# Last pass of an attention backward: every slab product is ordered behind a store copy on VectorE

## The chip, the cores and the metric

The kernel runs on one core of a Trainium2 chip. TensorE (PE), VectorE (DVE), ScalarE (ACT), GpSimd (POOL) and SyncE (SP) each run their own instructions in order; data moves between HBM and the on-chip memory through 16 DMA engines. In this kernel SP's queue issues all loads and POOL's queue all stores. The metric is the device time of one execution in microseconds (us); three executions of the kernel before took 1945.61, 1946.26 and 1947.33 us, median 1946.26.

## The reference

One token passes through two identical layers, each an attention over a long cache and a dense block; then the gradients of all inputs are computed from `grad_out`.

```python
# A: 32 query heads, 4 key/value groups, 65536 cached positions, head size 128, x of 1024
q = (x @ wq);  scores = q @ k.T * Dh**-0.5;  p = softmax(scores);  o = p @ v;  return o @ wo
# B: squared ReLU
h = x @ w1 + b1;  r = max(h, 0);  return (r*r) @ w2 + b2

x = x + A(layernorm(x));  x = x + B(layernorm(x))
x = x + A(layernorm(x));  x = x + B(layernorm(x))
out, vjp = jax.vjp(f, A_x, A_k_cache, A_v_cache, A_wq, A_wo, B_w1, B_b1, B_w2, B_b2)
return (out, *vjp(grad_out))
```

The gradients of the two caches are as large as the caches themselves: 64 MB each in bfloat16. The same weights and caches serve both layers, so the gradients of the two layers are summed.

## The kernel before, in words

The kernel makes four passes over the caches: two forward (one for each layer), one backward for the later layer, and a last one (`attn_bwd4`, L1289) that does the backward of the earlier layer together with the cache gradients of both. Dense stages lie between. Only the last pass is touched by the change.

The last pass goes through 256 items, 64 for each of the four groups; an item (`c8`) is 8 chunks of 128 positions. Four items make a block of 32 chunks, 1 MB of K or V. A block lies in one slot of an arena of 20 slots in on-chip memory (`Slot`, L318). Which slot a block, a weight slab or a staged output gets is decided when the program is written out; a load into a slot waits, in SP's queue, for the last reader of what lay there.

For each item the stages of the pipeline (L1476) do the following. `vT` (L1337) transposes V on PE and copies the result out (`kt`, mostly DVE). `vS` (L1365) multiplies it with the output gradients and, once per block, DVE writes the product `X` (L1403). `eT` and `xT` transpose the weights and `X` (`xt`). `dV8` and `dK8` call `outer16` (L1418): two outer products into PSUM (`ps_gg`), each of which `evac` (L150) copies into the staged output slot, by a running estimate of load on ACT (L161) or on DVE (L164); when the slot is full, POOL issues the store. These copies are called store copies here. `k8` (L1445) multiplies K with `X`. The first seven V blocks are already transposed from the pass before, so the transposes of V run over the other 228 items.

Beside this runs background work (`Background`, L777): the other outer products of the weight gradients, and `g_rowdots` (L577), a product of a weight slab with a vector. It comes six times in this pass, each for one group: three times on `wo` (for the output gradient of the next group) and three times on `wq` (a part of the gradient of x). Each needs two loads of 1 MB, four slab rows in each; a slab row is multiplied on DVE with the vector spread over all partitions (L598, a "product": 48 in the pass), and ACT sums the result (L587). The products are numbered 1 to 48 here, so that each job has eight, the first four on its first slab and the next four on its second one. As written, the second slab is requested after the fourth product, and eight waiting steps (one for each item) come before the fifth:

```python
            elif kc % 4 == 0:
                for _ in range(steps):
                    yield "wait"
            t = mvs.tile([P, n], BF, name="mv_t", tag="mv_t", bufs=2)
            nc.vector.tensor_tensor(out=t[:, :], in0=slab, in1=vbc[:, :], op=ALU.mult)
```

The order on the engines in the last pass isn't the order of writing. The earlier passes are issued as written (`manual_schedule`, L1177 and L1284), but the last pass is left to a scheduler, which orders each engine's instructions when the program is built, by its own estimate of when operands are ready. So it can place a product earlier among DVE's instructions than it was written, if by that estimate its slab has landed and DVE is free. On the chip each engine then keeps to the built order and waits at an instruction whose operand isn't there.

Of the kernel before, what the change touches and what calls it, by code (L numbers as in the profile page):

```python
# [3 lines left out]

# [9 lines left out]
ALU = mybir.AluOpType  # L14
# [6 lines left out]
def kernel(  # L21
# [24 lines left out]
    nc = tc.nc  # L46
# [98 lines left out]
    def add_load(act=0.0, dve=0.0, pe=0.0):  # L145
        load["act"] += act
        load["dve"] += dve
        load["pe"] += pe

    def evac(out, in_, kind="bf"):  # L150
        n = 1
        for d in in_.shape[1:]:
            n *= d
        ca = 0.17 + n * 0.00083
        cd = 0.13 + n * (0.00105 if kind == "f32" else 0.00054)

        if PS["pass4"] and kind == "bf":
            ca += 1.5
        if kind == "kta" or kind != "kt" and load["act"] + ca <= load["dve"] + cd:
            load["act"] += 0.17 + n * 0.00083  # L160
            nc.scalar.copy(out=out, in_=in_)  # L161
        else:
            load["dve"] += cd
            nc.vector.tensor_copy(out=out, in_=in_)  # L164


    def col_from_dram(v1d, n, name):
        nj = n // P
        rows = tmp.tile([nj, P], BF, name="rows_c", tag="rows_c")
        nc.sync.dma_start(out=rows[:], in_=v1d.rearrange("(j p) -> j p", p=P))  # L170
        pt = ps_mv([P, nj], BF)
        nc.tensor.transpose(pt[:, :], rows[:, :], ident_b[0:nj, 0:nj])
        col = vec.tile([P, nj], F32, name=name)
        nc.vector.tensor_copy(out=col[:], in_=pt[:])
        return col
# [383 lines left out]
    def g_bcast_vec(vcol, nj):  # L559
        pt = ps_mv([nj, P], F32)  # L560
        nc.tensor.transpose(pt[:, :], vcol, ident_f[:, :])
        yield
        rows = tmp.tile([32, P], BF, name="bc_rows")
        nc.vector.tensor_copy(out=rows[0:nj, :], in_=pt[:, :])
        vbc = mvs.tile([P, nj * P], BF, name="vbc", tag="vbc", bufs=1)
        yield
        for j0 in range(0, nj, 4):
            pg = ps_gg() if PS["pass4"] else ps_tr([P, 512], F32)
            for jj in range(4):
                nc.tensor.matmul(pg[:, jj * P:(jj + 1) * P], lhsT=ident_b[0:nj, j0 + jj:j0 + jj + 1].to_broadcast([nj, P]),  # L570
                                 rhs=rows[0:nj, :], start=True, stop=True)
            nc.scalar.copy(out=vbc[:, j0 * P:(j0 + 4) * P], in_=pg[:, 0:512])
            add_load(act=0.6)
            yield
        return vbc

    def g_rowdots(slab_it, nk, vcol, nj, finish, name):  # L577
        n = nj * P
        y = vec.tile([P, nk], F32, name=name)
        nc.gpsimd.memset(y[:], 0.0)  # L580
        vbc = None
        due = None
        steps = 8 if PS["pass4"] else WAIT_STEPS

        def total(t, kc):
            def f():
                nc.scalar.activation(out=t[:, :], in_=t[:, :], func=ACTF.Copy, accum_out=y[:, kc:kc + 1])  # L587
            return f
        for kc, slab in slab_it:
            if vbc is None:  # L590
                vbc = yield from g_bcast_vec(vcol, nj)
                for _ in range(steps - WAIT_STEPS + 1):
                    yield "wait"
            elif kc % 4 == 0:
                for _ in range(steps):
                    yield "wait"
            t = mvs.tile([P, n], BF, name="mv_t", tag="mv_t", bufs=2)
            nc.vector.tensor_tensor(out=t[:, :], in0=slab, in1=vbc[:, :], op=ALU.mult)  # L598
            add_load(dve=0.1 + n * 0.00054, act=0.42 + n * 0.00083)
            if due is not None:  # L600
                due()
            due = total(t, kc)
            yield
        due()
        yield
        r = finish(y[:, :])
        if r is not None:
            yield from r
        yield
# [679 lines left out]
    def attn_bwd4(p, La, Lb, on_group, bg, stack, end=()):  # L1289
# [128 lines left out]
        def outer16(name, out, key, xt, gg, j1):  # L1418

            if j1 == 0:  # L1420
                state[key] = Slot(name, True)
            stg = state[key].t[:, :].rearrange("p (j d) -> p j d", d=DH)
            for m in range(2):
                pg = ps_gg()
                for h in range(2):
                    nc.tensor.matmul(pg[:, 512 * h:512 * h + 512], lhsT=xt[64 * h:64 * h + 64, j1 // 8 + m, :],  # L1426
                                     rhs=gg[64 * h:64 * h + 64, :, :].rearrange("p a b -> p (a b)"),
                                     start=True, stop=True, tile_position=(64 * h, 0))
                jj = j1 + 8 * m
                evac(stg[:, jj:jj + 8, :].rearrange("p j d -> p (j d)"), pg[:, :], kind="f32")  # L1430
            if j1 + 16 == J:
                nc.gpsimd.dma_start(out=out, in_=stg)
                state.pop(key).free(stored=True)
# [522 lines left out]
```

## Time and profile before

| | |
|---|---|
| median of three executions | 1946.26 us |
| profiled execution, its time and its span | 1939.92 us, 1938.1 us |
| busy: PE, DVE, ACT, POOL | 1585.2, 1170.3, 1044.9, 142.2 us |
| bytes through the DMA engines | 787.63 MB, mean 406 GB/s |
| last pass, about | 1214 to 1938 us of the span |
| products in the last pass | 48, median 681 ns |
| DVE idle before products in the last pass | 34.1 us, of which 33.3 us on slabs |
| loads of one block in the last pass, issue to landing | K 15.9 us, V 13.2 us (medians) |

Times in the profile's rows count from the start of the span. In a row of the timeline the first two numbers are start and duration; "L598" is the line in the kernel; what stands in square brackets is the time for which the engine did nothing before this instruction, and what ended that. "issue" there means that the profile shows no data that came in; where a wait on a semaphore stands in the queue ahead of the instruction, the idle time is that wait's. In a table of windows a row gives, for each engine, busy time and instructions, then the granted TensorE clock, the share of the 16 DMA engines that was busy, and GB/s.

### The profile page before, as it was taken

Reading aid. Unit: us, or ns where it says so; the run is one execution under the profiler, and the core shown is the slowest. Engines: PE = TensorE matmul, PEld = TensorE weight load, DVE = VectorE, ACT = ScalarE, POOL = GpSimd, SP = SyncE. Lnnn points to the kernel's source line nnn. Section 1 sums busy time; section 2 is a strip of 40 time slices with the busy share of each in tenths; the row PEclk is TensorE's granted clock in tenths of the full one; section 3 lists DMA queues with packets and bytes.
Section 4 is the critical chain, followed back from the end, with each engine's and each line's share of the span. In section 5 each row is a group of like instructions: output and inputs, shape, how many; then the busy total and the mean of one; then the engine's idle time right before and its main releaser. Section 6 shows DMA issues by size and latency. Waiting matters only on the chain. (4 is left out here: it accounts for less than half of the span.)

```text
span 1938.1 us, 66986 instructions
## 1 busy us (share of the span) xinstructions
PE 1585.2 (82%) x30199; PEld 1301.4 (67%) x30199; DVE 1170.3 (60%) x2453; ACT 1044.9 (54%) x1617; POOL 142.2 (7%) x321
## 2 busy tenths in 40 slices
PE   6878778688777888977787898889997987697987
PEld 6878777678777877877776886555554654454554
DVE  5655555255555554545454567777775886685876
ACT  3444334245433545445363455766875885575775
POOL 0000000000000000000000001121111211121211
PEclk9999899689999999998899999898997998797998
DMA  9999999999999998999999988999999999899998
GB/s 393 427 425 425 429 427 415 391 407 423 427 425 429 428 422 309 377 425 429 426 424 421 408 314 308 425 424 389 425 424 413 419 424 424 345 419 397 424 422 352
DMA packets 107149, 787.63 MB, mean 406 GB/s; under 512 B 9440, under 2 KB 16622, under 8 KB 42222
## 3 DMA queue, kind: packets, MB, share of 16 engines
q1 hardware_dynamic: 82782, 617.65, 77.2%
q0 software_dynamic: 24080, 165.70, 20.5%
q8 instruction: 236, 3.87, 0.7%
q14 instruction: 51, 0.42, 0.1%
HBM read 617.62 MB, written 165.69 MB: 404 GB/s over the span
## 5 line engine op out<-in xcount | busy, mean ns | idle before, releaser
L164 DVE COPY kt<-ps_tr 128x1024 bf16<-128x1024 bf16 x724 | 496.3, 688 | 429.0 <-PE ps_tr L1024 244.0
L161 ACT CAST arena<-ps_gg 128x1024 bf16<-128x1024 f32 x457 | 444.4, 1011 | 185.0 <-PE ps_gg L1426 137.9
L1024 PE MATMUL ps_tr<-ident_b,arena 128*128 128x128 bf16 x3840 | 308.2, 225 | 36.9 <-DMA arena<-in_A_k_cache_dram 27.5
L161 ACT COPY kt<-ps_tr 128x1024 bf16<-128x1024 bf16 x164 | 171.0, 1046 | 186.1 <-PE ps_tr L1216 103.3
L164 DVE CAST arena<-ps_gg 128x1024 bf16<-128x1024 f32 (+2 forms) x186 | 222.2, 1195 | 77.1 <-PE ps_gg L1426 34.5
L1024 PEld LDWEIGHTS <-arena 128*128 128x128 bf16 x3840 | 232.9, 101 | 44.7 <-DMA arena<-in_A_k_cache_dram 30.3
L1126 PE MATMUL ps_acc<-arena 128*128 128x64 bf16 (+4 forms) x4096 | 205.6, 196 | 60.2 <-DMA arena<-in_A_v_cache_dram 45.1
L1426 PE MATMUL ps_gg<-GG,xt 64*128 64x512 bf16 x1024 | 210.6, 409 | 43.3 <-DVE arena L164 28.3
L1345 PE MATMUL ps_tr<-ident_b,arena 128*128 128x128 bf16 x1824 | 177.4, 232 | 33.7 <-DMA arena<-in_A_v_cache_dram 30.7
L1126 PEld LDWEIGHTS <-arena 128*128 128x128 bf16 x4096 | 159.9, 100 | 66.1 <-DMA arena<-in_A_v_cache_dram 48.7
L1042 PE MATMUL ps_sc<-L_qpad,kt 128*128 128x64 bf16 (+7 forms) x3584 | 183.0, 194 | 16.3 <-issue 8.3
L1107 ACT ACTIVATE arena<-S_sb,L_negm 128x128 bf16<-128x128 f32 x256 | 165.5, 1002 | 55.7 <-DVE L_negm L1092 42.2
L1216 PE MATMUL ps_tr<-ident_b,arena 128*128 128x128 bf16 x1920 | 154.3, 226 | 44.3 <-DMA arena<-in_A_v_cache_dram 43.5
L1345 PEld LDWEIGHTS <-arena 128*128 128x128 bf16 x1824 | 116.8, 103 | 90.7 <-issue 55.2
L1042 PEld LDWEIGHTS <-kt 128*128 128x128 bf16 x3584 | 152.6, 100 | 20.2 <-issue 8.8
L1216 PEld LDWEIGHTS <-arena 128*128 128x128 bf16 x1920 | 117.1, 101 | 48.8 <-DMA arena<-in_A_v_cache_dram 46.1
L1457 PEld LDWEIGHTS <-arena 128*128 128x128 bf16 x2048 | 92.2, 101 | 57.8 <-issue 39.9
L1107 ACT ACTIVATION_READ_ACCUMULATOR arena<-S_sb,L_negm 128x1 f32 x256 | 127.9, 500 | 0.0
L1426 PEld LDWEIGHTS <-xt 64*128 64x128 bf16 x1024 | 64.5, 94 | 90.1 <-issue 52.3
L587 ACT ACTIVATE mv_t<-mv_t 128x1024 bf16<-128x1024 bf16 x96 | 102.1, 1065 | 35.8 <-DVE mv_t L598 35.8
L1382 PE MATMUL ps_sc<-DOB,kt 128*128 128x64 bf16 (+3 forms) x1824 | 112.3, 197 | 0.1
L1270 PE MATMUL ps_acc<-dsT,arena 128*128 128x64 bf16 (+7 forms) x2048 | 103.1, 194 | 11.3 <-DMA arena<-in_A_k_cache_dram 7.8
(317 smaller groups left out, 2154.0 us busy)
## 6 DMA issues: line engine op xcount, KB each, us to landing
arena<-in_A_k_cache_dram SPq DMA_DIRECT2D x82, 2048.0 KB, 21.7
arena<-in_A_v_cache_dram SPq DMA_DIRECT2D x79, 2048.0 KB, 21.7
out_dram<-arena POOLq DMA_DIRECT2D x149, 1024.0 KB, 16.2
arena<-in_A_v_cache_dram SPq DMA_DIRECT2D x84, 1024.0 KB, 14.2
arena<-in_A_k_cache_dram SPq DMA_DIRECT2D x84, 1024.0 KB, 14.6
arena<-in_A_wo_dram SPq DMA_DIRECT2D x22, 1024.0 KB, 19.6
arena<-in_B_w_dram SPq DMA_DIRECT2D x21, 1024.0 KB, 9.2
arena<-in_A_wq_dram SPq DMA_DIRECT2D x18, 1024.0 KB, 18.0
```

Of the source, the lines that this page charges most:

```text
L161: nc.scalar.copy(out=out, in_=in_)
L164: nc.vector.tensor_copy(out=out, in_=in_)
L587: nc.scalar.activation(out=t[:, :], in_=t[:, :], func=ACTF.Copy, accum_out=y[:, kc:kc + 1])
L1024: nc.tensor.transpose(pt[:, i, :], kb8[:, i, :], ident_b[:, :])
L1042: nc.tensor.matmul(state["ps_s"][:, s:s + w, :].rearrange("p a b -> p (a b)"), lhsT=kt[:, i, :], rhs=L["qpad"][:, g, 0:w, :].rearrange("p ...
L1107: nc.scalar.activation(out=E(p, g, c0, SU)[:, :, h], in_=S[:, h, :], func=ACTF.Exp, bias=L["negm"][:, g, su, h:h + 1], scale=SCALE, accum_ ...
L1126: nc.tensor.matmul(ps_o[:, 0:w, :], lhsT=vb8[:, i, :], rhs=E(p, g, c, w), start=(c % SU == 0), stop=(c % SU == SU - 1), skip_group_check=True)
L1216: nc.tensor.transpose(pt[:, i, :], vb8[:, i, :], ident_b[:, :])
L1270: nc.tensor.matmul(ps_dq[:, 0:w, :].rearrange("p a b -> p (a b)"), lhsT=kb8[:, i, :], rhs=dsT[:, s:s + w, :].rearrange("p a b -> p (a b)") ...
L1345: nc.tensor.transpose(pt[:, i, :], vb8[:, i, :], ident_b[:, :])
L1382: nc.tensor.matmul(state["ps_dp"][:, s:s + w, :].rearrange("p a b -> p (a b)"), lhsT=vt[:, i, :], rhs=DOB[:, g, 0:w, :].rearrange("p a b - ...
L1426: nc.tensor.matmul(pg[:, 512 * h:512 * h + 512], lhsT=xt[64 * h:64 * h + 64, j1 // 8 + m, :], rhs=gg[64 * h:64 * h + 64, :, :].rearrange(" ...
```

## The change

`issue_after(i)` makes every instruction that is written inside its block, on the engine of `i`, come later than `i` in the built order of that engine. It adds no wait on the chip. With the change, `outer16` remembers its last store copy if that went to DVE (a copy on ACT leaves the earlier one remembered), and every product is ordered behind the copy remembered at the place where the product is written. Before the first such copy nothing is remembered, so the products of the earlier passes are as they were. The arithmetic, the number of instructions on each engine that compute or move data, the split of copies between ACT and DVE and the slots are the same; the built order in the last pass differs on all engines.

```diff
+    PIN = {"copy": None}
+    def mark_store_copy():
+        i = nc.cur_bb.bb.instructions[-1]
+        if i.engine == mybir.EngineType.DVE:
+            PIN["copy"] = i
+    @contextmanager
+    def behind_store_copy():
+        if PIN["copy"] is None:
+            yield
+        else:
+            with tc.issue_after(PIN["copy"]):
+                yield
...
             t = mvs.tile([P, n], BF, name="mv_t", tag="mv_t", bufs=2)
-            nc.vector.tensor_tensor(out=t[:, :], in0=slab, in1=vbc[:, :], op=ALU.mult)
+            with behind_store_copy():
+                nc.vector.tensor_tensor(out=t[:, :], in0=slab, in1=vbc[:, :], op=ALU.mult)
...
                 jj = j1 + 8 * m
                 evac(stg[:, jj:jj + 8, :].rearrange("p j d -> p (j d)"), pg[:, :], kind="f32")
+                mark_store_copy()
```

More of the change, by code (lines that the diff above doesn't have):

```diff
@@ L1 @@
-from contextlib import ExitStack
+from contextlib import ExitStack, contextmanager
 from collections import deque
```

## The prediction, made before the changed kernel was run

> **What bounds the kernel now.** I read the page first, then stretches of the last pass, then who waits for whom there, then the timelines at the longest waits. The page's slices show the DMA engines at 0.99 and more almost everywhere, at 424 to 429 GB/s, and no other engine full. So the last pass lasts as long as its transfers, plus the time in which the DMA engines have too little to do. I looked for that time in windows of 2 us. The bytes that a dip lacks against 425 GB/s give its price.
>
> ```profile
> DMA  9999999999999998999999988999999999899998
> GB/s 393 427 425 425 429 427 415 391 407 423 427 425 429 428 422 309 377 425 429 426 424 421 408 314 308 425 424 389 425 424 413 419 424 424 345 419 397 424 422 352
> ```
>
> In the last pass there are four dips ahead of the tail: 1314 to 1334 us (4.0 us of transfer missing), 1496 to 1510 (2.0), 1670 to 1698 (9.5) and 1780 to 1790 (3.1). The waits of DVE name what stands ahead of three of them: four waits of a product for its slab, 27.8 + 5.5 = 33.3 us.
>
> ```profile
> DVE kt L164 <- PE ps_tr L1345: 59.2, 50, 10.8
> DVE mv_t L598 <- issue: 27.8, 3, 14.0
> DVE mv_t L598 <- DMA arena<-in_A_wq_dram: 5.5, 1, 5.5
> ```
>
> The longest one, in the timelines of DVE, SP and PE, and then the windows:
>
> ```profile
> 1660.72 0.42 DVE L164 COPY xt<-ps_tr 128x512 bf16<-128x512 bf16 x1
> 1675.15 0.69 DVE L598 TENSOR_TENSOR mv_t<-arena,vbc 128x1024 bf16<-128x1024 bf16 x1 [14.02 <-issue]
> 1675.76 1.22 DVE L164 CAST arena<-ps_gg 128x1024 bf16<-128x1024 f32 x1
> ```
>
> ```profile
> 1655.77 0.38 SPq L462 DMA_DIRECT2D arena<-in_A_wq_dram  x1
> 1656.24 1.00 SPq L365 DMA_DIRECT2D arena<-in_A_v_cache_dram  x1
> 1657.55 24.26 SPq L365 DMA_DIRECT2D arena<-in_A_k_cache_dram  x2
> ```
>
> ```profile
> 1677.03 0.61 PE L1426 MATMUL ps_gg<-GG,xt 64*128 64x512 bf16 x2 [12.17 <-DVE arena L164]
> ```
>
> ```profile
> 1656.00:1658.00 2.00, 1.59 (x24) 0.91 (x21) 2.00 (x4) 2.00 (x4) 0.00 (x0) 1.00 0.98 406
> 1670.00:1672.00 2.00, 0.00 (x0) 0.00 (x0) 0.00 (x0) 0.00 (x0) 0.00 (x0) 0.50 0.85 359
> ...
> 1674.00:1676.00 2.00, 0.00 (x0) 0.00 (x0) 0.85 (x2) 0.12 (x1) 0.00 (x0) 0.50 0.07 30
> 1676.00:1678.00 2.00, 0.97 (x7) 0.53 (x7) 2.00 (x3) 2.00 (x4) 0.00 (x0) 0.50 0.07 29
> ...
> 1684.00:1686.00 2.00, 2.00 (x40) 1.70 (x37) 0.59 (x1) 2.00 (x4) 1.62 (x4) 0.85 0.99 418
> ```
>
> The reader sees a ring close. The slab was requested at 1655.77 and DVE stands at its product from 1661 to 1675. The store copy behind the product is late, so PE waits for PSUM from 1665. No slot comes free, SP's next K load is held until about 1682, and POOL has nothing to store. What was in flight lands, and the DMA engines run dry from 1670. The product waited for the transfers; for the 9.5 us after that, the transfers waited for the product.
>
> **The change, part by part.** Instructions are the same: 48 products of 681 ns before and after, and no wait is added, so their busy time costs 0 more. What changes is the built order, which can be read without running it. I count it in items of V transposed on PE (0 to 228), taking each engine's instruction at the last V transpose that it needs, directly or through what stands ahead of it.
>
> *Waits that go.* Between the request of a second slab and its first product lay 7, 10, 7, 3, 2 and 3 items in the six jobs. In the new order it is 18, 18.6, 15, 14.9, 14 and 15. The waits in the trace are at jobs 3 to 6: 5.45, 3.66, 14.02 and 10.08 us, the jobs with the short distances. The pass makes 31 blocks between products 9 and 41, 1385.67 to 1757.94 us: 12.0 us a block, 3.0 an item. So 14 items are 42 us. A slab's 1 MB lands in a median of 22.6 us (`wq`) or 9.9 us (`wo`), so all four waits go. Bounds for what they are worth: nothing, if the DMA engines stay the limit as at the wait of 3.66 us, which left them at full share; 33.2 us if each wait was lost whole. I take the missing transfer behind them, 2.0 + 0 + 9.5 + 3.1 = 14.6 us, since that is what the transfer-bound end can win. A stall that goes makes ACT's sum of a product (26.4 us of waits for products in this pass) punctual too; that is inside the 14.6.
>
> *The wait that the product takes over.* The copy ahead of it was on DVE before and waits for its matmul as before; the products now stand one by one behind copies, with their slab long landed. DVE's queue behind them (the copies of `kt` and `xt`, for which PE waits) gains nothing new to wait for: 0, bounded above by the 5.5 us that the job with the longest distance among those that waited had (7 items, job 3), and not below 0, since the copy itself isn't changed.
>
> *Slots held longer.* The slot of a second slab is read out later, and SP's load into it can be issued later: at item 21 for 15, 71 for 63, 100 for 92, 133 for 128, 164 for 152 and 199 for 188. Its neighbours in SP's in-order queue are released there too, so what counts is the distance to its own use. That stays at 5.1 items or more (15 us, against a V load's 13.2) in all jobs but the first, where a V block is left with 3.1.
>
> *SP, POOL and PE reordered.* SP's queue differs in 17 places and POOL's in 31. By the same count, three places in the first group become tight in the new order and have at most one load behind them that could fill the DMA engines: a K block held by the fourth product (2 items), that V block (3.1) and a K block with no load behind it (3 items). DVE makes 20 copies of `kt` between 1231 and 1304 us, 3.65 us an item there. With landings of 15.9 and 13.2 us, PE would wait 8.6 + 1.9 + 4.9 = 15.4 us. Before, 33.2 us of waiting made 14.6 us of missing transfer, a share of 0.44; I take 6.8 us for the 15.4, since these are waits of the same kind, and bound it by 0 and 15.4. The dip at 1314 comes from a store copy that waited 4.9 us for its slot's earlier store, and the order of stores around it changes: between 4.0 us won and 4.0 us lost, taken as 0.
>
> *The tail.* The last products move from block 52 to 55 of 64; the sum that needs them is due after the last block: 0, as 9 blocks (108 us) cover it.
>
> *Sum.* 1939.9 - 14.6 + 6.8 = 1932.1 us against the profiled execution. That one is 6.3 us faster than the median of the three, and I assume the same gain there: 1946.3 - 7.8 = 1938.5 us.
>
> **The rivals.** *The transfers stay the bound and nothing is won*: the dips come back at the next tight place, as the same 787.63 MB have to move. For it: the wait of 3.66 us cost no transfer, and neither did the wait of 10.8 us for a V block near 1629. Against: 1670 to 1684, at a share of 0.50. It gives 1946 us. [...]
>
> *Slower: K blocks arrive late.* The new order has, ahead of the tail, seven K loads with 3 items or fewer between release and use (1, 2, 2, 2, 3, 3, 3) where the old one has five (2, 3, 3, 3, 3). At 3.0 us an item and 15.9 us to landing that is 63.3 us of waiting against 37.5, 25.8 us more. If all of it were missing transfer, the time would be 1946.3 - 14.6 + 25.8 = 1957.5 us. It decides once more than 57% of it (14.6 of 25.8) is. For it: PE waits in order at such a block, and three of the seven lie in the first group. Against: most have three or more loads issued behind them, and the row below shows 15.9 us of such waits where the count says 37.5.
>
> ```profile
> PE ps_acc L1457 <- DMA arena<-in_A_k_cache_dram: 15.9, 4, 10.7
> ```
>
> *That the order isn't changed* can be left out: all 48 products stand later in DVE's built order.
>
> **How the numbers follow.** Faster as summed: 0.62, with 1927.7 (14.6 and 4.0 won, nothing lost) to 1947.1 (15.4 lost) as its own range. Nothing won: 0.13. Slower by late K blocks: 0.25. What a measurement of this kernel can tell from no change is about 0.2%, 3.9 us. The predicted time is 1938.5 us. The range, 1928 to 1954 us, takes the likeliest case to its lower end and most of the slower one. Faster, same and slower have 0.62, 0.13 and 0.25.
>
> **What would show it.** Right: DVE's waits for slabs fall from 33.3 us to under 5, and no 2 us window between 1340 and 1890 us is under 300 GB/s for long; SP has no load held for 24 us there. The first 100 us of the pass show PE waiting for K, some 15 us more. Wrong: the waits for slabs go and dips of the same size stand elsewhere, behind K loads or behind store slots; or the products wait as before.

## The result, and the profile after

The changed kernel is slower: 1960.24 us (median of six, 1954.04 to 1969.65) against 1945.93 us for the kernel before beside it, a ratio of 1.0081 with a 95% interval of 1.0054 to 1.0108. The prediction was 1938.5 us, faster with a chance of 0.62, and the time lies outside its range of 1928 to 1954 us. The profiled execution took 1954.04 us with a span of 1952.0 us, 14 us above the one shown of before, so it can be read for the difference.

The page's slices of the changed kernel, the DMA engines' share and GB/s in 40 equal parts of the span:

```profile
DMA  9999999999999998999999988999999999999997
GB/s 394 426 427 426 427 428 413 397 410 425 428 426 427 428 420 297 388 426 428 424 424 423 399 320 328 413 372 406 417 373 423 424 425 424 370 374 424 412 422 304
```

Up to the last pass nothing is slower; its first load is issued at 1202.2 us (1205.6 before). From there to the end it takes 749.7 us and before it took 732.5, so all of the loss, 17.2 us, is in the last pass. Counted as in the prediction, by what windows of 2 us lack against 425 GB/s from 1200 us to the end, 46.9 us of transfer are missing and 31.9 were before. The difference of 15.0 us makes up most of the 17.2. (Such sums shift by a few tenths with the place at which the first window starts.)

Who waits in the last pass, for DVE's products and for PE's loads; the columns are the sum, the number and the longest. First PE's row for V blocks in the kernel before (the prediction shows the one for K blocks, 15.9 us, and those for slabs), then the changed kernel:

```profile
PE ps_tr L1345 <- DMA arena<-in_A_v_cache_dram: 30.7, 10, 10.7
```

```profile
DVE mv_t L616 <- ACT mv_t L604: 0.3, 1, 0.3
PE ps_tr L1363 <- DMA arena<-in_A_v_cache_dram: 48.6, 7, 12.8
PE ps_acc L1476 <- DMA arena<-in_A_k_cache_dram: 41.3, 9, 13.9
```

The products wait for no slab any more: 33.3 us before, none now. PE's waits for V blocks rose from 30.7 to 48.6 us and those for K blocks from 15.9 to 41.3 us. So 33.3 us went from DVE and 43.3 us came to PE. The three longest waits for V, from PE's timeline:

```profile
1300.56 0.29 PE L1363 MATMUL ps_tr<-ident_b,arena 128*128 128x128 bf16 x1 [12.76 <-DMA arena<-in_A_v_cache_dram]
1421.71 0.50 PE L1363 MATMUL ps_tr<-ident_b,arena 128*128 128x128 bf16 x3 [11.19 <-DMA arena<-in_A_v_cache_dram]
1687.73 0.50 PE L1363 MATMUL ps_tr<-ident_b,arena 128*128 128x128 bf16 x3 [11.72 <-DMA arena<-in_A_v_cache_dram]
```

Each stands ahead of a dip: 1304 to 1328 us (7.2 us of transfer missing), 1428 to 1460 (5.6) and 1690 to 1730 (11.7). The first two lie in jobs 1 and 2, where the kernel before had one dip of 4 us. There the slots held longer by products are reloaded: the first is the V block in the slot of job 1's second slab, the second the one in the slot of job 2's first slab. The third is where DVE stood 14.0 us at a slab before; now the product is later, and PE stands at the V block that was requested right behind that slab. SP's timeline and the windows there:

```profile
1664.49 0.38 SPq L479 DMA_DIRECT2D arena<-in_A_wq_dram  x1
1665.65 0.33 SPq L382 DMA_DIRECT2D arena<-in_A_v_cache_dram  x1
1673.02 1.69 SPq L382 DMA_DIRECT2D arena<-in_A_k_cache_dram  x2
1676.04 0.85 SPq L382 DMA_DIRECT2D arena<-in_A_v_cache_dram  x2
1699.51 0.33 SPq L382 DMA_DIRECT2D arena<-in_A_k_cache_dram  x1
1712.71 0.33 SPq L382 DMA_DIRECT2D arena<-in_A_v_cache_dram  x1
```

```profile
1684.00:1688.00 4.00, 0.27 (x3) 0.24 (x3) 0.00 (x0) 0.00 (x0) 0.00 (x0) 0.50 1.01 426
1688.00:1692.00 4.00, 4.00 (x33) 1.95 (x31) 2.76 (x4) 2.02 (x2) 0.00 (x0) 0.50 0.95 399
1692.00:1696.00 4.00, 4.00 (x28) 2.08 (x28) 2.40 (x4) 2.02 (x2) 0.53 (x1) 0.50 0.34 143
1696.00:1700.00 4.00, 4.00 (x31) 2.04 (x29) 1.83 (x5) 1.93 (x2) 0.62 (x1) 0.50 0.65 272
1700.00:1704.00 4.00, 4.00 (x35) 2.29 (x33) 2.39 (x5) 2.03 (x2) 0.85 (x2) 0.50 0.82 262
...
1708.00:1712.00 4.00, 4.00 (x30) 1.90 (x28) 2.52 (x4) 1.98 (x2) 0.53 (x1) 0.50 0.20 79
```

The block was issued at 1665.65 and its data came at 1687.7, 22 us later. The DMA engines are full until then and run dry after: from 1690 to 1712 PE is busy all the time, but at a granted clock of 0.50, and the next loads, which wait for slots that PE has to read out, are issued at 1699.5 and 1712.7. PE stood for 11.7 us here, where it had stood for 12.2 us behind DVE before. The wait only changed its engine, and the dip behind it was larger (11.7 us of transfer against 9.5).

### The profile page after: what moved, and what is told of

It reads as the page before. It is cut to its first block, busy times and chain, and to the rows that moved or that the text cites. A ratio compares the mean times of both kernels' runs of the same rounds, so it can differ in the third digit from the quotient of the medians.

```text
span 1952.0 us, 66951 instructions
## 1 busy us (share of the span) xinstructions
PE 1584.1 (81%) x30199; PEld 1298.4 (67%) x30199; DVE 1170.3 (60%) x2453; ACT 1045.2 (54%) x1617; POOL 144.9 (7%) x321
## 5 line engine op out<-in xcount | busy, mean ns | idle before, releaser
L1363 PE MATMUL ps_tr<-ident_b,arena 128*128 128x128 bf16 x1824 | 178.4, 233 | 51.7 <-DMA arena<-in_A_v_cache_dram 48.6
L1363 PEld LDWEIGHTS <-arena 128*128 128x128 bf16 x1824 | 118.3, 103 | 107.1 <-issue 55.8
L1060 PEld LDWEIGHTS <-kt 128*128 128x128 bf16 x3584 | 153.6, 100 | 20.4 <-ACT kt L161 9.5
L1476 PE MATMUL ps_acc<-X,arena 128*128 128x64 bf16 (+3 forms) x1536 | 94.3, 197 | 34.0 <-DMA arena<-in_A_k_cache_dram 34.0
L1400 PEld LDWEIGHTS <-kt 128*128 128x128 bf16 x1824 | 83.0, 101 | 44.3 <-issue 42.6
## 6 DMA issues: line engine op xcount, KB each, us to landing
arena<-in_A_wq_dram SPq DMA_DIRECT2D x18, 1024.0 KB, 13.8
```

The source lines that it names most:

```text
L1060: nc.tensor.matmul(state["ps_s"][:, s:s + w, :].rearrange("p a b -> p (a b)"), lhsT=kt[:, i, :], rhs=L["qpad"][:, g, 0:w, :].rearrange("p ...
L1363: nc.tensor.transpose(pt[:, i, :], vb8[:, i, :], ident_b[:, :])
L1400: nc.tensor.matmul(state["ps_dp"][:, s:s + w, :].rearrange("p a b -> p (a b)"), lhsT=vt[:, i, :], rhs=DOB[:, g, 0:w, :].rearrange("p a b - ...
L1476: nc.tensor.matmul(ps_dq[:, 0:w, :].rearrange("p a b -> p (a b)"), lhsT=kb8[:, i, :], rhs=X[:, s:s + w, :].rearrange("p a b -> p (a b)"), ...
```

## The experiments

Ratios are to the kernel before on the same chip, with 95% intervals; the microseconds are the difference of the medians. The last pass is counted in the profiled execution from its first load to the end, missing transfer as above, the waits for V and K are PE's, and those for slabs are the products' on DVE. These columns come from one execution of each kernel, which can lie some us from its median: those of the kernel before and of the changed one are 6 us under theirs, that of run 2 is 5.5 us under and that of run 9 is 2.0 us over. The theories go by letters, as the expectations explain them: A, B and C in run 1, D in run 5 (the products' late places on DVE make the loss by themselves), E and F in run 9. Runs 13 and 14 repeat runs 5 and 10, which had one tile more on the chip (below).

The scheduler takes part in these experiments: an edit that leaves it free also moves instructions on engines that the edit doesn't name. Counted in the built programs as the fewest that must be taken out for the rest to stand in the same order, the changed kernel moves 22 loads on SP, 343 of 2403 instructions on DVE and 7164 of 60148 on PE. Runs 9 and 14, which hold all orders, and run 15 move none. Run 16 moves 11 loads and 16 instructions on PE, and on DVE none. In runs 1 to 4, 6 to 8 and 11 to 13 between 10 and 344 instructions on DVE moved, and between 387 and 7177 on PE (run 11 against the changed kernel, the others against the kernel before), so these show what a whole built order costs and not one cause by itself.

| kernel | ratio | us | last pass | missing | waits V, K | slabs |
|---|---|---|---|---|---|---|
| before | | | 732.5 | 31.9 | 46.6 | 33.3 |
| changed | 1.0081 (1.0054 to 1.0108) | +14.3 | 749.7 | 46.9 | 89.9 | 0 |
| 1: jobs 1, 2 bound | 1.0048 (1.0035 to 1.0061) | +9.2 | 744.5 | 45.8 | 59.0 | 33.4 |
| 2: jobs 3 to 6 bound | 1.0067 (1.0046 to 1.0088) | +10.6 | 739.2 | 39.6 | 73.2 | 0 |
| 3: second slabs bound | 1.0060 (1.0048 to 1.0072) | +11.3 | 746.4 | 46.3 | 78.9 | 0 |
| 4: first slabs bound | 1.0030 (1.0020 to 1.0039) | +5.7 | 739.8 | 38.1 | 84.0 | 8.1 |
| 6: bound, slabs not read | 1.0136 (1.0100 to 1.0171) | +28.5 | 755.7 | 55.8 | 101.1 | 0 |
| 7: unbound, slabs not read | 1.0087 (1.0067 to 1.0107) | +18.2 | 750.6 | 51.1 | 95.8 | 0 |
| 8: bound loosely, jobs 4 to 6 | 1.0033 (1.0020 to 1.0045) | +7.0 | 742.5 | 40.1 | 77.7 | 12.9 |
| 9: slabs not read, order kept | 1.0005 (0.9993 to 1.0016) | +0.2 | 737.0 | 37.6 | 75.5 | 0 |
| 11: changed, two V blocks first | 1.0052 (1.0036 to 1.0068) | +9.7 | 750.2 | 48.8 | 85.0 | 0 |
| 12: SP's order | 1.0124 (1.0098 to 1.0150) | +21.7 | 754.9 | 56.2 | 69.3 | 21.2 |
| 13: slots held, not bound | 1.0092 (1.0077 to 1.0106) | +16.8 | 754.6 | 54.3 | 71.0 | 26.1 |
| 14: two stalls on DVE | 1.0079 (1.0062 to 1.0095) | +13.8 | 748.1 | 47.9 | 34.6 | 32.1 |
| 16: SP's order, jobs 3 to 6 | 1.0068 (1.0054 to 1.0082) | +13.9 | 744.8 | 45.8 | 61.4 | 18.6 |

### Where in the pass the loss is made (1 to 4)

```diff
+            with behind_store_copy() if PIN["job"] <= 2 else ExitStack():    # 1; PIN["job"] > 2 in 2
+            with behind_store_copy() if kc >= 4 else ExitStack():            # 3; kc < 4 in 4
```

> Only the products of jobs 1 and 2 (16 of 48) are bound; jobs 3 to 6 stand as in the kernel before. Theory A (a bound product reads its slab out later, so the slot of the slab comes free later and the V or K block loaded into it, with everything behind it on SP, is late): the loss was made in jobs 1 and 2, where the missing transfer rose from 4.0 to 15.4 us, so this kernel has nearly all of the loss: 1946 + 11.4 = 1957 us, with PE waits of 11 to 13 us for V blocks between 1290 and 1430 us, and DVE still waiting about 33 us for slabs of jobs 3 to 6. Theory B (the long slab waits of jobs 3 to 6 only move on to PE, and that is where the loss is): no loss, 1943 to 1949 us. Theory C (the loss is the tail's, where the missing transfer rose from 8.2 to 14.0 us): 1946 to 1952 us with the dip after 1900 us as large as in the changed kernel.

> Only the products of jobs 3 to 6 (32 of 48) are bound, the jobs where DVE waited 33.3 us for slabs; jobs 1 and 2 stand as in the kernel before. Theory A: the missing transfer of these jobs went from 14.3 to 12.9 us when they were bound, so the time is that of before less 1.4 us: 1943 to 1948 us, with the waits of products for slabs under 2 us, and a V block or K block for which PE waits 8 us or more in the place of each long one. Theory B: the loss of the changed kernel stands here, 1955 to 1960 us. The prediction's own sum, were only its second part wrong: 1946 - 14.6 = 1931 us. Theory C: 1949 to 1952 us, from a larger dip in the tail.

> Only the products of the second slab of each job (24 of 48) are bound. The first slab's slot then comes free as in the kernel before; the second one's as late as in the changed kernel. Theory A: of the three dips of jobs 1 and 2 in the changed kernel, the two that follow a block held by the fourth product (2.2 + 5.8 us) go, and the one that follows the V block held by the eighth (7.4 us) stays: 1946 + 11.4 - 8.0 = about 1949 us, PE waiting some 12 us for that V block near 1300 us. Theory B: as the changed kernel, 1957 to 1960 us, since all slab waits of jobs 3 to 6 go here too.

> Only the products of the first slab of each job (24 of 48) are bound; by the built order the second slab is then used 12, 12, 11, 9, 4 and 9 items after its request (18, 19, 15, 15, 14 and 15 in the changed kernel, 7, 10, 7, 3, 2 and 3 before). Theory A: the two dips that follow blocks held by the fourth product (2.2 + 5.8 us) stay, the one held by the eighth (7.4 us) goes, and most of the slab waits are gone (one of some 10 us is left, at 4 items): 1946 + 8.0 - 4.0 = about 1950 us. Theory B: the fewer slab waits are left the slower, so slower than before by some two thirds of the loss: about 1955 us.

Both halves lose: 9.2 us with the first two jobs bound, 10.6 us with the other four. Together that is more than the 14.3 us of the whole, so the two don't simply add. In run 1 the dips of jobs 1 and 2 are those of the changed kernel (2.6, 8.5 and 4.9 us at 1264, 1308 and 1432) behind waits of 13.5 and 11.3 us for the same two V blocks, as theory A says. Run 2 is a miss for it: theory A gave no loss there, theory B all of it, and it is some three quarters. The rows of run 2 for DVE's products and PE's loads:

```profile
DVE mv_t L618 <- ACT mv_t L606: 0.4, 2, 0.2
PE ps_tr L1365 <- DMA arena<-in_A_v_cache_dram: 21.0, 5, 9.1
PE ps_acc L1478 <- DMA arena<-in_A_k_cache_dram: 52.2, 10, 12.0
```

The 33.3 us of slab waits are gone here too, and PE's waits for K alone have grown by 36.3 us. Run 3 missed as well (1949 us expected by theory A, 1955.84 measured, which is nearer to theory B's 1957 to 1960). Run 4 has the time that was expected (1950.26 us) but not the dips: 3.3 us at 1258, and none near 1430. Any part of the binding costs something, and no part gains.

### What the slab waits were worth (6, 7, 9)

The products of the last pass read the broadcast vector and not their slab, so nothing waits for a slab and its slot is free when it has landed; the gradients' row sums are left out. Run 6 does this with the products bound, run 7 with the kernel before, run 9 with the kernel before and all engines' orders held as they were.

```diff
-                nc.vector.tensor_tensor(out=t[:, :], in0=slab, in1=vbc[:, :], op=ALU.mult)
+                nc.vector.tensor_tensor(out=t[:, :], in0=vbc[:, :] if PS["pass4"] else slab, in1=vbc[:, :], op=ALU.mult)
...
+        for order in orders.values():          # 9: order of issue before, for PE, DVE, ACT, POOL, SP
...
+            for a, b in zip(chain, chain[1:]):
+                tc.add_manual_dep(b, a.name, NoSync, reason="order")
```

> Bound as in the changed kernel, but the 48 products of the last pass read the broadcast vector in the place of their slab (the weight gradients' row sums are left out, so the output is another). All slabs are still loaded; nothing waits for them and their slots come free when they have landed. Theory A: the held slots are gone and so are the slab waits, so the dips of jobs 1 and 2 that follow V blocks (7.2 and 5.6 us) go: 1946 us or less, 1931 us if the slab waits were worth the prediction's 14.6 us. Theory D: the products stand on DVE as in the changed kernel, so 1957 to 1963 us.

> The kernel before, with the same edit as the run before it: the products of the last pass read the broadcast vector in the place of their slab (row sums left out). This is what the slab waits and the time from landing to reading cost the kernel before, without any other edit. The prediction's second part: the dips of 1.7, 9.4 and 2.9 us go, 1946 - 14 = 1932 us. Its rival (the transfers stay the bound, a dip comes back at the next tight place): 1943 to 1947 us.

> The kernel before with the products of the last pass reading the broadcast vector and not their slab (row sums left out), and with every engine's order of issue in the last pass (PE, DVE, ACT, POOL, SP) held as it is in the kernel before. So only the dependence on the slabs is gone: their four waits, and nothing is moved. This measures the prediction's second part by itself. The prediction: 14.6 us of missing transfer goes, 1944 - 14.6 = 1929 us. Theory E (conserved waiting: the last pass has to move 300 MB, 703 us at 425 GB/s, and PE is busy for 619 us of it, so some 100 us of waiting must stand somewhere; what is taken from DVE comes back as PE's waits for V and K blocks): 1940 to 1950 us, DVE's 33 us of slab waits 0, PE's waits for V and K up from 46.6 us by 25 us or more. Theory F (a slab wait on DVE is even the cheaper place for it): 1950 us or more, as the run without slabs and without a held order (1961 us).

Run 9 decides: with the four waits taken away and nothing moved, the time is the same, 1.0005 (0.9993 to 1.0016). They were worth nothing, and not 14.6 us. Who waits in run 9, and PE at the place of the longest slab wait:

```profile
PE ps_tr L1347 <- DMA arena<-in_A_v_cache_dram: 47.1, 11, 10.7
PE ps_acc L1459 <- DMA arena<-in_A_k_cache_dram: 28.4, 7, 9.4
```

```profile
1683.46 0.93 PE L1347 MATMUL ps_tr<-ident_b,arena 128*128 128x128 bf16 x7 [10.71 <-DMA arena<-in_A_v_cache_dram]
1690.57 0.93 PE L1459 MATMUL ps_acc<-X,arena 128*128 128x64 bf16 x14 [4.22 <-DMA arena<-in_A_k_cache_dram]
```

PE's waits for V and K went from 46.6 to 75.5 us: 28.9 of the 33.3 us came back. At the longest wait it is again the V block requested right behind the slab. It came 24.3 us after its issue (1659.17 in SP's timeline; PE went on at 1683.46), and the dip behind it is 12.6 us, where it was 9.5 behind the slab wait. In the kernel before that V block was issued at 1656.24, and the trace, which records when each of a load's 16 pieces lands, has the last one at 1677.39, 0.4 us after PE went on at 1677.03. In run 9 PE gets from the instruction at which it stood before to this block in 6.0 us. So without the slab it would have stood again from about 1671 to 1677.4, as worked out from these rows. What could be won is the work that PE did between 1677 and 1685, where it reached the block. Run 9 wins a part of that: its 24.3 us from the issue to PE going on with the block are 29 us in the kernel before. It then stands 4.2 us for a K block (second row above), and nearly all of the gain is gone. This fits theory E: the pass moves 298.86 MB, 703 us at 425 GB/s, and PE is busy for 618.6 us from 1200 us on, so at least 84 us of waiting must stand somewhere.

Runs 6 and 7 missed both their theories, at +28.5 and +18.2 us. They aren't clean: with slots free that early, the scheduler moved 23 and 13 loads on SP. Run 6, with the products bound, is 10.3 us slower than run 7, though no slab is waited for in either; with so much moved this is no price of the late products, but it doesn't speak for 0 either. In run 7 the V block for job 1's second slab went from the tenth to the fifth place of the queue, where it waits for that slab to land, and the K block behind it was issued 21.4 us after the pass's first load (16.2 before). That pointed to the queue's order, which runs 11, 12 and 16 take up.

### Slots held, or loads in another order (11, 12, 13, 16)

```diff
+            if kc % 4 == 3 and PIN["copy"] is not None:      # 13: no product is bound
+                with behind_store_copy():
+                    nc.vector.tensor_copy(out=sixt[:, 0:1], in_=slab[:, 0:1])
...
+        for a, b in zip(chain, chain[1:]):     # 11, 12, 16: SP's loads in a given order
+            tc.add_manual_dep(named[b], named[a].name, _mybir.DependencyInfo(_mybir.DependencyClass.NoSync, _mybir.DependencyReason.DATA), reason="load order")
```

> As the run that held the slots alone (no product bound, one column of each slab copied behind the store copy that the changed kernel binds its product to), but the column goes to a constant's tile that nothing reads any more, so no tile is added. In that run the last pass took 751.2 us from its first load, against 732.5 before and 749.7 in the changed kernel. If holding the slots makes the changed kernel's loss: 1945 + 14 to 19 = 1959 to 1964 us. If the added tile made it: 1943 to 1947 us.

> The kernel before, no product bound, but SP's loads in the last pass are held in the order that they have in the changed kernel. Of the change's two effects on the loads (a slot comes free later; the queue is put in another order) only the second is left. If the order alone makes the loss of jobs 1 and 2: 1944 + 9 = 1953 us or more, with the long waits for the two V blocks near 1300 and 1420 us. If the late slots make it: 1943 to 1947 us.

> The kernel before, no product bound, SP's loads held in the order that they have where only jobs 3 to 6 are bound (12 loads moved). The run with these jobs bound lost 10.6 us. If the order of the loads makes that: 1953 to 1957 us. If the late slots make it: 1943 to 1948 us.

> The changed kernel with two loads moved in SP's queue and the rest of SP's order held: the V block of the second slab's slot in job 1 goes ahead of the four loads that are needed later (three V blocks, one K block), and the V block of the first slab's slot in job 2 ahead of one. The waits of 12.8 and 11.2 us for these two blocks stood ahead of dips of 7.2 and 5.6 us. Theory A (the late slots, through SP's in-order queue, make the loss of jobs 1 and 2): the first one is issued some 9 us earlier and the second 2 to 3 us, the waits fall to 4 and 8 us, and the time from 1960 to 1950 to 1955 us. Theory E: the wait comes back at another block and the time stays at 1957 us or more.

Run 13 holds the slots and leaves the products where they were, with their waits (26.1 us). It loses 16.8 us, as much as the changed kernel. So a loss of this size needs no late product on DVE. It is no measure of the held slots by themselves: 15 loads on SP and 198 instructions on DVE moved too, and its V blocks in jobs 1 and 2 have less room than those of the changed kernel (1.1, 3.5 and 2.1 items against 3.1, 5.1 and 4.1, as expected for run 5, whose order it has). Its rows, with the slab waits still there and V's grown by 14 us:

```profile
DVE mv_t L615 <- issue: 25.4, 3, 12.3
PE ps_tr L1365 <- DMA arena<-in_A_v_cache_dram: 44.8, 9, 12.0
PE ps_acc L1478 <- DMA arena<-in_A_k_cache_dram: 26.2, 5, 10.7
```

Runs 12 and 16 free the slots as early as before, but issue the loads in the order of the changed kernel and of run 2. They lose 21.7 and 13.9 us, at least as much as the kernels whose order they have (14.3 and 10.6). In run 16 that is the order of the loads: hardly anything else moved. So for jobs 3 to 6 this order is enough: a load that the kernel before issues early into a slab's slot (the V block in the slot of job 5's second slab, at item 152, 20 items ahead of its use) then comes at item 164. In its rows PE's waits for K blocks rise from 15.9 to 37.4 us, while 18.6 us of slab waits stay:

```profile
DVE mv_t L598 <- issue: 12.2, 2, 8.8
DVE mv_t L598 <- DMA arena<-in_A_wq_dram: 6.4, 2, 6.0
PE ps_tr L1345 <- DMA arena<-in_A_v_cache_dram: 24.0, 9, 6.5
PE ps_acc L1457 <- DMA arena<-in_A_k_cache_dram: 37.4, 9, 9.6
```

Run 12 is not the order of the loads alone: the scheduler also moved 201 instructions on DVE and 3732 on PE. What the order costs in jobs 1 and 2 is not shown by itself.

Held slots and order were not taken apart further. Bound products with SP's order of before were not run: SP's queue would stand at a block whose slot a product releases, the product would stand behind a store copy, and that copy would need a block behind the first one. By this argument, which wasn't tried, the late slots force the other order.

Run 11 takes up one link of this. In the changed kernel the V block for job 1's second slab stood behind three V blocks and a K block that are needed later. Ahead of them, it comes in time, and the transfer missing between 1200 and 1500 us goes from 18.6 to 14.6 us. The time went from +14.3 to +9.7 us, but the intervals of the ratios overlap, so the gain itself isn't certain, and 58 instructions on DVE and 1602 on PE moved with the two loads. Part of the wait came back at the next block of the queue, a K block (8.1 us):

```profile
1315.99 0.55 PE L1476 MATMUL ps_acc<-arena 128*128 128x64 bf16 x7 [8.10 <-DMA arena<-in_A_k_cache_dram]
```

### The price of a stall on DVE (14)

```diff
+            if PS["pass4"] and kc == 4:                      # all orders held, as in 9
+                PS["jobs"] = PS.get("jobs", 0) + 1
+                if PS["jobs"] in (1, 2):
+                    nc.vector.tensor_reduce(out=sixt[:, 0:1], in_=vbc[:, :].unsqueeze(1).to_broadcast([P, 14, n]), op=ALU.add, axis=mybir.AxisListType.XY)
```

> As the run with two stalls of some 14 us on DVE (ahead of the fifth products of jobs 1 and 2, every engine's order held as before), without the added tile. In that run the last pass was 14.1 us longer. The prediction's price (a stall loses half): 1945 + 14 = 1959 us. Conserved waiting: 1945 to 1950 us. A stall lost whole: 1973 us.

DVE's timeline shows the first stall, and the windows what follows (the second took 15.08 us):

```profile
1231.33 15.06 DVE L603 TENSOR_REDUCE sixt<-vbc 128x1 f32<-128x14336 bf16 x1
```

```profile
1244.00:1248.00 4.00, 0.35 (x4) 0.35 (x4) 4.00 (x4) 0.97 (x2) 0.00 (x0) 0.50 0.99 416
1248.00:1252.00 4.00, 4.00 (x40) 2.46 (x37) 3.75 (x5) 1.19 (x3) 0.77 (x2) 0.50 0.12 47
1252.00:1256.00 4.00, 3.97 (x56) 2.53 (x54) 3.54 (x7) 3.82 (x6) 0.37 (x1) 1.00 0.63 262
```

The ring closes as the prediction described it: PE stops 14.0 us, the DMA engines stay full until 1248 and then run dry. The two dips are 8.1 and 7.1 us, a share of 0.50 of the 30.1 us, and the kernel is 13.8 us slower. Most of the other half is taken out of PE's waits for V and K, which fall from 46.6 to 34.6 us:

```profile
PE ps_tr L1355 <- DMA arena<-in_A_v_cache_dram: 22.0, 6, 10.7
PE ps_acc L1467 <- DMA arena<-in_A_k_cache_dram: 12.6, 4, 9.8
```

Those for slabs stay, at 32.1 us for 33.3. Of these, 3.2 us are put down to ACT in DVE's timeline:

```profile
1590.21 0.69 DVE L606 TENSOR_TENSOR mv_t<-arena,vbc 128x1024 bf16<-128x1024 bf16 x1 [3.19 <-ACT mv_t L589]
```

ACT's sum had ended at 1589.3, and the last piece of the slab landed at 1590.13. So the prediction's price for a stall is near to what two added ones cost in jobs 1 and 2, and wrong for the four that run 9 takes away. That the difference is the load behind, late there and not here, is read from the rows around the longest of the four; it wasn't tried at the others.

### Versions that might beat the kernel before (8, 17, 18)

Run 8 binds only the second slabs of jobs 4 to 6, each to the fourth-last store copy written ahead of it. Runs 17 and 18 bind nothing and change the eight waiting steps ahead of the fifth product to 7 and to 3 (those ahead of the first go with them).

```diff
+            PIN["last"].append(i)                            # 8, in mark_store_copy: the fourth-last copy
+            if len(PIN["last"]) > 3:
+                PIN["copy"] = PIN["last"].popleft()
...
+            with behind_store_copy() if PIN["job"] >= 4 and kc >= 4 else ExitStack():
...
-        steps = 8 if PS["pass4"] else WAIT_STEPS
+        steps = 7 if PS["pass4"] else WAIT_STEPS             # 17; 3 in 18
```

> Only the products of the second slabs of jobs 4 to 6 (12 of 48) are bound, and each behind the fourth-last store copy written ahead of it and not the last: by the built order they come 8, 8 and 7 items after the slab's request (3, 2 and 3 before, 14.9, 14 and 15 in the changed kernel), which is 21 to 24 us at 3.0 us an item, about a landing. No K load ahead of the tail is left with fewer than 3 items. The prediction's second part, with no slot held for long: the waits of 3.7, 14.0 and 10.1 us go or shrink to under 3 us, and 1946 - 12.3 = 1934 us. Theory A with conserved lead (a slot held longer is taken from the lead of the V and K blocks, so a wait of the same size comes back on PE): 1943 to 1949 us, with PE waits for V or K near 1690 and 1790 us grown by some 10 us.

> The kernel before with the products of the last pass written 7 steps behind the request of their slab and not 8, no binding. In the built order the distances from release to use of the V and K blocks sum to 863 items (848 before, 795 in the changed kernel). If this sum sets the price, 0.26 us an item: 4 us faster than before, 1939 to 1942 us. If it only went along with something else: anything, and about as likely slower as faster.

> The same with 3 steps: the sum is 864 items, so by the same price 4 us faster than before, 1939 to 1942 us. If the sum isn't the cause: anything, and not the same as with 7 steps.

Run 8 cut the slab waits to 12.9 us (9.7 of them at job 3, which it doesn't bind), and lost 7.0 us; PE's waits grew by 31.1 us. Runs 17 and 18 are misses: 1.0027 (1.0013 to 1.0041) and 1.0019 (1.0005 to 1.0032), slower where the sum of the distances said faster. That sum goes along with the loss in the kernels that it was found on, and doesn't predict it.

### One tile more (5, 10, 15)

The first forms of runs 13 and 14 wrote to a small tile of their own. They came out at 1.0169 (1.0151 to 1.0188) and 1.0129 (1.0114 to 1.0145), with the last pass 18.7 and 14.1 us longer, close to their later forms (22.1 and 15.6), and the last pass started 18.5 and 15.4 us later, though nothing is changed ahead of it.

```diff
+                tail = mvs.tile([P, 1], BF, name="mv_h", tag="mv_h", bufs=2)      # 5, in the place of sixt
+                    stall = vec.tile([P, 1], F32, name="stall")                   # 10, in the place of sixt
+    spare = vec.tile([P, 1], F32, name="spare")                                   # 15
+    nc.vector.memset(spare[:], 0.0)
```

> No product is bound. A copy of one column of the slab is bound in their place, behind each slab's fourth product: the products keep their early places and their waits, but each slab's slot is held about as long as in the changed kernel (12 short copies more on DVE). By the built order the V blocks held by the second slabs of jobs 1 and 2 and by the first of job 2 are left with 1.1, 3.5 and 2.1 items between release and use (3.1, 5.1 and 4.1 in the changed kernel). Theory A (the held slots alone make the loss): slower than before by at least the changed kernel's 14 us, 1960 us or more, with PE waits of over 10 us for V blocks near 1300 and 1430 us and DVE's waits for slabs still near 33 us; 1975 us if the waits for slabs cost 14.6 us as the prediction has it. Theory D (the products' late places on DVE themselves make the loss, by what they displace): as before, 1944 to 1948 us.

> The kernel before, all engines' orders in the last pass held as they are, plus one reduction of some 14 us on DVE right ahead of the fifth product of job 1 and of job 2, where DVE had no wait: two stalls of the size of the longest slab wait. The prediction's price for a stall (0.44 to 0.5 of missing transfer): slower by 12 to 14 us, 1957 us. Theory E (the waiting is conserved): most of the 28 us comes off PE's waits for V and K, and the time is 1944 to 1950 us. If a stall is lost whole: 1972 us.

> The kernel before with one more tile of 128x1 numbers, set to zero once and never read. If the tile alone made the two earlier runs slower ahead of the last pass (full slices of 420 to 422 GB/s there, against 425 to 427): about 1945 + 13 = 1958 us, the last pass as long as before and starting 13 to 15 us later. Otherwise 1945 us.

With the tile alone the kernel is at 1.0078 (1.0053 to 1.0103). The last pass starts 17.4 us later and is 3.2 us longer. The tenth to fourteenth slices of the page show 423, 427, 425, 429 and 428 GB/s before. Here, in the same row of the page of run 15, they show 420 to 424:

```profile
GB/s 388 422 422 418 423 423 409 383 400 420 424 420 423 423 413 305 358 421 424 420 418 420 407 301 303 416 420 410 419 424 409 419 424 424 346 423 393 425 422 323
```

So full slices move about 1% less there. In the built program the arena of slots starts at byte 48896 of each partition in the kernel before and at 48928 in run 15 (48960 in run 5).

## Why the prediction was wrong, step by step

**Waits that go.** That they go is right: 33.3 us to none. What they are worth, 14.6 us, is the step that failed first; run 9 measured 0 (between 1.4 us gained and 3.1 us lost, by its interval). The dips behind the waits were real, but the working asked only what each wait held up, and not what PE would meet next if it didn't stand there. At the longest wait that was the V block right behind the slab in the same queue, equally late. The prediction's first rival (the dips come back at the next tight place) described this and was given 0.13. The row quoted against it, the DMA engines at a share of 0.50 from 1670 to 1684, shows only that transfer was missing, not that it would be there without the wait. But a stall of DVE isn't worth nothing everywhere: in run 14 30.1 us of added stall cost 13.8 us.

**The wait that the product takes over.** Taken as 0. For it: the products wait for no copy worth a row (0.3 us in the row above), and run 13 loses as much with no late product. But no run has the late places alone with all other orders held, so whether DVE's work behind them costs nothing stays open.

**Slots held longer.** This was costed at nothing by the distance from release to use, "5.1 items or more (15 us, against a V load's 13.2)". Run 13 holds the slots and loses 16.8 us, as much as the whole change, though other orders moved with it. What failed is the 13.2 us. It is a median over the pass, and these blocks aren't median. The one left with 3.1 items was issued at 1279.6 and came at 1300.5, 20.9 us, with four loads issued in the 10 us ahead of it. With 13.2 us its wait came out as 1.9 us; with 20.9 the same count gives 9.6, and 12.8 was measured. The one with 4.1 items, in the slot of job 2's first slab, took 19.7 us, and no wait was counted for it; 11.2 us was measured. The neighbours in the queue were named in the prediction and left without a price.

**SP, POOL and PE reordered.** 15.4 us more of PE waiting at three places was expected, 6.8 us of it lost. At the three places PE waited 5.9 us (K), 12.8 (V) and less than 3 (K). But PE's waits for loads grew by 43.3 us over the pass, for V as well as K. The share of 0.44 is near run 14's 0.50; the sum of the waits was mis-sized, since what is taken from DVE comes back. The loss of jobs 3 to 6 (run 2) wasn't in the working at all, and run 16 shows that the order of the loads there is enough for it. The dip at 1314 behind a late store, taken as 0, did go, and the larger one behind the V block stands in its place.

**The tail.** Taken as 0. Missing transfer from 1900 us on rose from 8.2 to 13.8 us in the profiled executions. But it is 11.0 us in run 9, which is no slower, so the binding can't be charged with all of it; what of it is the change's stays open.

**The rival "K blocks arrive late".** It computed 25.8 us more of K waits and the trace shows 25.4; its time, up to 1957.5 us, is the nearest of those worked out. That the two numbers agree is in part luck: the levels were 22 us too high, 63.3 counted against 41.3 in the trace and 37.5 against 15.9, run 9 has 12.5 us more of such waits with no block moved, and the waits for V blocks, which the rival left out, grew by 17.9 us. It was held down to 0.25 by an argument from the row of before (15.9 us of such waits where the count says 37.5). In run 9, where only DVE's waits are gone, the same row is 28.4 us: it was low in the kernel before while DVE did the waiting. Its condition, that more than 57% of the added waiting must be missing transfer to lose on balance, assumed that the 14.6 us were won.

Of the marks that the prediction set, one came true: slab waits under 5 us. Another did in part: in the first 100 us of the pass PE's waits of over 2 us for loads rise from 6.4 to 18.6 us, but those for K, which were forecast, only from 3.2 to 5.9. The others came out on the side of "wrong": windows under 300 GB/s between 1692 and 1712, SP issuing nothing from 1676.9 to 1699.5, and dips of the same size behind V and K loads.

What is shown: the slab waits were worth nothing (run 9), and the order of the loads in jobs 3 to 6 by itself makes a loss of 13.9 us (run 16). What is argued: that held slots and late V blocks make the loss of jobs 1 and 2, since runs 1, 11, 12 and 13 moved other engines' instructions with them. What the other engines' orders, the late products and the lower clock (below) add wasn't measured by itself. Why the order of before is this good stays open too. Every kernel here that moves loads in the last pass lost, also those with more distance between release and use.

## What to carry to other kernels

In this pass, where transfers fill nearly all of the time (a DMA share of 0.99 from 1200 us on in the kernel before), a wait on a load was worth only what the engines could do before they met the next late load of the same queue (run 9: 33.3 us of waits gone, and the time the same at +0.2 us). So look at the blocks requested right behind the awaited one before a price is put on the wait. A reader that is moved later holds its buffer longer, and here the queue of loads behind it changed with it (22 loads moved); cost this with the landing time at that place in the queue, and not with the median over the stage. To price a wait, take away what it depends on with all orders of issue held, as run 9 does; an edit that also lets the scheduler reorder measures the reordering (run 7 against run 9: 18 us). Compare the built orders of all engines before a difference is put down to the edit.

## What the runs showed of the hardware that was not expected

The granted clock stayed low long after a wait. After PE's wait of 11.72 us for a V block in the changed kernel the windows show 0.50 from 1687.7 to past 1712, with PE busy in all of them; the wait of 12.17 us behind DVE in the kernel before left it at 0.50 until about 1685, 8 us after PE went on. In run 14 it was back at 1.00 within 5 us of a wait of 14.0 us (PE went on at 1247.64; row of 1252 above). So after waits of 11.7, 12.2 and 14.0 us it stayed at 0.50 for 25 us and more, 8 us and under 5; what differs between them wasn't tried. Counted by windows of 2 us from 1200 us on, the clock was at 0.50 for 161 us in the kernel before, 180 in the changed one and 183 in run 9, which is no slower than the kernel before; what it adds to the loss wasn't separated. In the changed kernel PE is the slower side while it lasts, busy in all of each window from 1688 to 1712, and the DMA engines are at 79 to 272 GB/s in four of these six windows.

Another was the unread tile of run 15: 16 us for a tile of 128x1 numbers, with about 1% less transfer in the full slices ahead of the last pass (420 to 424 GB/s against 423 to 429). In the built program the arena lies 32 bytes further on. Whether that makes it, or something else that moved with the tile, wasn't tried: no run puts the tile in and the arena back.

The last was one late piece in 16. Of the slab requested at 1655.77 in the kernel before, 15 pieces had landed by 1669.85 and the last at 1675.07; of the V block behind it, 15 by 1672.26 and the last at 1677.39. Over the loads of the pass in the kernel before the last piece comes a median of 0.5 us after the one ahead of it. So 5 of the 14 us at that slab went to a single piece; why it was late wasn't tried.
